# Fifteen small loads behind the last weights of a decode step, into a tile that nothing reads

## The chip, the cores and the metric

One Trainium2 chip, one of its cores. The metric is the device time of one execution in microseconds; a kernel's time is the median over its runs. The profile is one execution taken by the hardware profiler; its times count from the first instruction.

## What is computed

One decode step for two sequences (B = 2, one token each, D = 576), a sliding-window attention and a dense squared-ReLU layer side by side on the same normalised input:

```python
xn = _layernorm(x)
# attention: 32 query heads, 16 cached heads of 128, the last W = 2048 positions of the caches
q = (xn @ wq)                       # heads of 128
p = softmax(q k^T * 128 ** -0.5)
attn = (p v) @ wo
# dense layer, F = 4608
h = relu(xn @ w1 + b1) ** 2
dense = h @ w2 + b2
out = x + attn + dense
```

All inputs and the output are bf16. The caches' windows, 2 x 16 heads x 2048 positions x 128 for keys and for values, and the four weight matrices make up nearly all of the bytes: the profile counts 53.6 MB read from memory.

## The kernel before, in words

The attention is cut into eight units `u`: four groups of four cached heads, times two sequences. A unit has one 2 MB key tile and one 2 MB value tile (`issue_kv`, L106), each one DMA over 128 partitions. The order of the work on an engine is the order of the program: `step(u)` transposes the keys of a unit on TensorE, takes scores and softmax, and weights the values of unit `u - 2` in between. `mlp_h` makes the hidden layer from w1 after `step(6)`. At the end stand `step(NU - 1)`, the last two units' values (`pv_all`), and the output products: `out_acc` adds wo, then w2 in two halves, into one PSUM tile `out_ps`. `fin_sb` (L456) is its copy in SBUF, and the store at L457 writes the result. An earlier store (L455) of the same bytes to `out` takes its data from w2b; the later one writes over it.

All large loads are issued by SP, in one queue: first keys, wq and values, as buffers become free; then w1; then, after `mlp_h`, wo (L119), the first half of w2 (w2a, L438), and the second half in four pieces: nine row groups (w2b, L439), then six, two and one into the tile w2c (L441). x, b1, b2 and the two stores are issued by ACT.

The framework places the waits. DMAs of both queues complete on eight semaphores, given out in rotation in the order in which the framework schedules them, so a DMA waits for the one that used its semaphore before. Where a transfer writes bytes that an earlier one writes or that an engine still reads, it waits for that too. The program ends on SP with waits for the semaphores of the DMAs, and then a barrier of all engines (the line of the kernel's end, L483 in the profile).

The loads at the end, as they stand:

```python
    nc.sync.dma_start(out=w2a_sb[:], in_=w2_rows[0])
    nc.sync.dma_start(out=w2b_sb[:], in_=w2_rows[1, :, 0:R9 * D])
    for r0, r1 in W2P:
        nc.sync.dma_start(out=w2c_sb[:, (r0 - R9) * D:(r1 - R9) * D], in_=w2_rows[1, :, r0 * D:r1 * D])
```

Of the kernel before, what the change touches and what calls it, by code (L numbers as in the profile page):

```python
# [9 lines left out]
BF16 = mybir.dt.bfloat16  # L10
# [6 lines left out]
def kernel(  # L17
# [14 lines left out]
    nc = tc.nc  # L32
    P = 128
# [53 lines left out]
    w2pool = ctx.enter_context(tc.tile_pool(name="w2pool", bufs=1))  # L87
# [92 lines left out]
    for t0, half, k0, n, pc in ((0, 0, 0, NK, 0), (0, 1, 0, NK, 1), (1, 0, 1, NK - 1, 1), (1, 1, 0, NK - 1, 0)):  # L180
# [11 lines left out]
                          in_=own[:].unsqueeze(2).to_broadcast([P, NC, WC]))  # L192
# [11 lines left out]
                          in_=ident[0:2 * NG4, 0:2 * NG4].rearrange("p (x g) -> p x g", g=NG4).unsqueeze(3)  # L204
# [53 lines left out]
    def transposes(u, g):  # L258
        k_f = k_tiles[u][:].bitcast(F32)
        kT_ps = psum.tile([P, JG * P], BF16, tag="kT", bufs=3, name=f"kT_ps_{u}_{g}")  # L260
        kT_f = kT_ps[:].bitcast(F32)
        for i in range(JG // 2):
            j = g * JG // 2 + i
            transpose(out=kT_f[:, i * P:(i + 1) * P], in_=k_f[:, j * P:(j + 1) * P], identity=ident_f[:])
        t, o = divmod(g, TG)
        if o == 0:
            kT_tiles[(u, t)] = ktpool.tile([P, TG * JG * P], BF16, tag="kT_sb", name=f"kT_{u}_{t}")
        kT = kT_tiles[(u, t)][:, o * JG * P:(o + 1) * JG * P]
        if g % 2 == 0:
            nc.scalar.copy(out=kT, in_=kT_ps[:])  # L270
        else:
            nc.vector.tensor_copy(out=kT, in_=kT_ps[:])  # L272

    def scores(u, t):
        tq, b = divmod(u, B)
        if t == 0:
            sc_tiles[u] = psum.tile([P, NJJ * 32], F32, tag="sc", bufs=2, name=f"sc_ps_{u}")
            matmul(sc_tiles[u][:], lhsT=far_h[:], rhs=is_h, start=True, stop=False, skip_group_check=True)
        sc_ps = sc_tiles[u]
        kT = kT_tiles.pop((u, t))[:].rearrange("p (j k c) -> p j k c", k=P, c=2)  # L280
        z = QZ * (1 - t)
        for c in range(2):
            for g in range(4):
                matmul(sc_ps[32 * g:32 * (g + 1), :], lhsT=qz[:, tq, b, c, z:z + SR],
                       rhs=kT[:, :, 32 * g:32 * (g + 1), c], start=False, stop=(t == NT - 1 and c == 1),
                       skip_group_check=True, tile_position=(0, 32 * g))

    def softmax(u):
        sc_ps = sc_tiles.pop(u)
        m1 = work.tile([P, 1], F32, tag="m1", name=f"m1_{u}")  # L290
        nc.vector.tensor_reduce(out=m1[:], in_=sc_ps[:], axis=AX.X, op=ALU.max)  # L291
        m2 = work.tile([P, NC], F32, tag="m2", name=f"m2_{u}")
        nc.vector.tensor_scalar(out=m2[:], in0=off[:], scalar1=m1[:, 0:1], scalar2=None, op0=ALU.add)  # L293
        gmax = work.tile([P, NC], F32, tag="gmax", name=f"gmax_{u}")
        nc.gpsimd.partition_all_reduce(gmax[:], m2[:], channels=P, reduce_op=ReduceOp.max)  # L295
        gown = work.tile([P, NC], F32, tag="gown", name=f"gown_{u}")
        bias = work.tile([P, 1], F32, tag="bias", name=f"bias_{u}")
        nc.vector.scalar_tensor_tensor(out=gown[:], in0=gmax[:], scalar=-scale, in1=own[:], op0=ALU.mult,  # L298
                                       op1=ALU.mult, accum_out=bias[:])
        p_sb = work.tile([P, NJJ * 32], BF16, tag="p_sb", bufs=1, name=f"p_{u}")  # L300
        o1 = keep.tile([P, Dh + 1], F32, tag="o1", name=f"o1_{u}")
        nc.scalar.activation(out=p_sb[:], in_=sc_ps[:], func=ACT.Exp, bias=bias[:, 0:1], scale=scale,  # L302
                             accum_out=o1[:, Dh:Dh + 1])
        pT = keep.tile([P, NJJ, SR], BF16, tag="pT", name=f"pT_{u}")
        nc.vector.transpose(out=pT[:].rearrange("p j r -> p (j r)"), in_=p_sb[:])  # L305
        pT_tiles[u] = pT
        o1_tiles[u] = o1
# [6 lines left out]
    def pv(u, part, parts):  # L314
        n = NJJ // parts
        if part == 0:
            o_tiles[u] = psum.tile([P, NS * Dh], F32, tag="o", name=f"o_ps_{u}")
        v = v_tiles[u][:].rearrange("p (t j s d) -> p j t s d", t=NT, s=2, d=Dh)
        for j in range(part * n, (part + 1) * n):
            g = j % 4  # L320
            matmul(o_tiles[u][32 * g:32 * (g + 1), :], lhsT=pT_tiles[u][:, j, :], rhs=v[:, j], start=(j < 4),
                   stop=(j >= NJJ - 4), skip_group_check=True, tile_position=(0, 32 * g))
        if part == parts - 1:
            pT_tiles.pop(u)

    def pv_end(u):
        tq, b = divmod(u, B)
        o_ps = o_tiles.pop(u)
        o1 = o1_tiles.pop(u)
        for k in range(NS):  # L330
            kw = dict(out=o1[:, 0:Dh], in0=o_ps[:, k * Dh:(k + 1) * Dh])
            if k == 0:
                nc.vector.tensor_scalar(scalar1=in_s[:, 0:1], scalar2=None, op0=ALU.mult, **kw)
            else:
                nc.vector.scalar_tensor_tensor(scalar=in_s[:, k:k + 1], in1=o1[:, 0:Dh], op0=ALU.mult, op1=ALU.add,  # L335
                                               **kw)

        def fin():
            op = psum.tile([P, Dh + 1], F32, tag="op", name=f"op_ps_{u}")
            pp = slice(32 * tq, 32 * (tq + 1))  # L340
            matmul(op[pp, :], lhsT=of_h[:], rhs=o1[:], start=True, stop=True, skip_group_check=True,
                   tile_position=(0, 32 * tq))
            linv = work.tile([P, 1], F32, tag="linv", name=f"linv_{u}")
            nc.vector.reciprocal(out=linv[pp, :], in_=op[pp, Dh:Dh + 1])
            om_t = work.tile([P, Dh], F32, tag="om", name=f"om_{u}")
            om = om_t[pp, :].rearrange("p (q r) -> p q r", r=WR)
            nc.vector.scalar_tensor_tensor(out=om, in0=op[pp, 0:Dh].rearrange("p (q r) -> p q r", r=WR),
                                           scalar=linv[pp, 0:1], op0=ALU.mult, op1=ALU.mult,
                                           in1=own_c[pp, :].unsqueeze(2).to_broadcast([32, WC, WR]))
            with nc.allow_low_precision(reason="sums of one term and zeros"):  # L350
                nc.vector.tensor_reduce(out=ws[pp, :, BS * b], in_=om.rearrange("p q r -> p r q"), axis=AX.X,  # L351
                                        op=ALU.add)

        return fin
# [32 lines left out]
    def step(u):  # L387
        fin = None
        w = u - 2
        with_pv = w >= 0  # L390
        for g in range(NG):
            transposes(u, g)
            if with_pv and g == 1:
                pv(w, 0, 2)
            if with_pv and g == 2:
                pv(w, 1, 2)
                fin = pv_end(w)
            if g == TG + 1:
                scores(u, 0)
            if g == TG + 2 and fin:  # L400
                fin()
        scores(u, 1)
        softmax(u)

    def pv_all(u):
        pv(u, 0, 1)
        pv_end(u)()
# [31 lines left out]
    nc.sync.dma_start(out=w2b_sb[:], in_=w2_rows[1, :, 0:R9 * D])  # L439
    for r0, r1 in W2P:  # L440
        nc.sync.dma_start(out=w2c_sb[:, (r0 - R9) * D:(r1 - R9) * D], in_=w2_rows[1, :, r0 * D:r1 * D])  # L441
    step(NU - 1)
    pv_all(NU - 2)
    pv_all(NU - 1)
# [43 lines left out]
```

## Time and profile before

| | |
|---|---|
| time, median of 2 runs | 134.19 us (134.15 to 134.24) |
| span of the profiled execution (first to last instruction) | 132.1 us |
| time of the profiled execution beside its span | the page gives the span alone; the median is 2.1 us above it |
| busy share of the span | PE 64%, DVE 48%, ACT 35%, POOL 4% |
| mean granted TensorE clock | 0.834 |
| bytes read, mean rate | 53.62 MB, 406 GB/s over the span |
| chain that ended last | DMA 78%, PE 15%, ACT 2%, the rest 1% and less each |

How to read the views: the chain that ended last is followed back from the last instruction, each step to what released it; its columns are start, length and what. The timeline has start, length, engine, line, operation, output and input of each instruction, and in brackets what ended the idle time before it. SPq and ACTq are the instructions by which SP and ACT hand over DMAs; their length is that of the issue, not of the transfer. In a row of waits stand who waited, for whom, how long in total, how often, and the longest. The rows of digits and of GB/s cut the stretch asked for into 40 equal slices.

### The profile page before, as it was taken

The page shows a single profiled execution, that of the slowest core. Times are in us where ns is not written, and L with a number is a line of the kernel's source. Part 1 is how long each engine was busy: PE and PEld are TensorE (multiplying, and loading weights), DVE is VectorE, ACT ScalarE, POOL GpSimd, SP SyncE. Part 2 cuts the span into 40 slices and gives each one's busy share as a digit, 9 for nine tenths or more (in the row PEclk, how much of TensorE's full clock was granted, in tenths as well). Part 3 has the DMA queues.
Part 4 walks back from the last instruction along what each step waited for, and adds up shares of the span by engine and source line. Part 5 has one row for each costly group of instructions (what it writes and reads, how often), then busy time and mean ns, then how long its engine had stood idle before and what let it go on. Part 6 is the DMA issues. An engine that isn't in the chain of part 4 may idle for free.

```text
span 132.1 us, 2285 instructions
## 1 busy us (share of the span) xinstructions
PE 84.6 (64%) x949; PEld 52.6 (40%) x949; DVE 63.2 (48%) x176; ACT 46.7 (35%) x67; POOL 4.9 (4%) x15
## 2 busy tenths in 40 slices
PE   0089319599589687697599787104819972739471
PEld 0069202286345353363455443002417640229360
DVE  7764400344557677396547687410075667550000
ACT  5725400339566085283256094200106632000000
POOL 5000000010010100100100100100000001000000
PEclk9999955959999999999779999855695999555955
DMA  4999899999999999999999999999999999899960
GB/s 160 397 437 526 369 388 442 422 432 432 429 432 422 442 417 427 437 432 437 432 427 414 437 488 402 445 424 405 427 427 442 468 435 458 376 408 418 418 255 1
DMA packets 3511, 53.76 MB, mean 407 GB/s; under 512 B 419, under 2 KB 558, under 8 KB 814
## 3 DMA queue, kind: packets, MB, share of 16 engines
q1 hardware_dynamic: 3456, 53.61, 95.2%
q8 instruction: 7, 0.11, 0.3%
q10 hardware_dynamic: 46, 0.02, 0.1%
q14 instruction: 2, 0.02, 0.0%
HBM read 53.62 MB, written 0.00 MB: 406 GB/s over the span
## 4 chain that ended last, share of the span: by engine, by line
DMA 78%; PE 15%; ACT 2%; SPq 1%; DVE 1%; issue 1%; ACTq 0%; DVEq 0%
DMA w<-in_B_w_dram 25%; DMA w2c<-in_B_w_dram 24%; DMA k<-in_A_k_cache_dram 16%; DMA wq<-in_A_wq_dram 13%; PE kT_ps L97 5%; PE h_ps L94 3%; PE q_ps L94 3%; PE sc_ps L94 2%; PE out_ps L94 1%; PE o_ps L94 1%; ACT kT L270 1%; DVE qrow L238 1%; SPq L106 0%; ACT qrow L238 0%; DVE qz L254 0%
## 5 line engine op out<-in xcount | busy, mean ns | idle before, releaser
L97 PE MATMUL kT_ps<-ident_f,k 128*128 128x128 f32 x256 | 41.4, 312 | 5.7 <-DMA k<-in_A_k_cache_dram 3.9
L97 PEld LDWEIGHTS kT_ps<-ident_f,k 128*128 128x128 f32 x256 | 32.9, 161 | 18.8 <-issue 9.9
L270 ACT COPY kT<-kT_ps 128x1024 bf16<-128x1024 bf16 x32 | 31.9, 1012 | 17.8 <-PE kT_ps L97 17.8
L272 DVE COPY kT<-kT_ps 128x1024 bf16<-128x1024 bf16 x32 | 21.8, 682 | 6.4 <-PE kT_ps L97 6.1
L94 PE MATMUL sc_ps<-kT,qz 128*32 128x512 bf16 x128 | 9.9, 388 | 6.7 <-DVE kT L272 4.7
L302 ACT ACTIVATE p<-sc_ps,bias 128x512 bf16<-128x512 f32 x8 | 5.5, 688 | 21.4 <-DVE gown L298 18.2
L94 PE MATMUL o_ps<-v,pT 128*32 128x512 bf16 x128 | 11.2, 429 | 0.0
L94 PEld LDWEIGHTS <-xnT 128*4 128x4 bf16 x108 | 3.5, 121 | 16.8 <-issue 15.2
L94 PE MATMUL h_ps<-w,xnT 128*4 128x288 bf16 x72 | 4.3, 429 | 8.0 <-DMA w<-in_B_w_dram 8.0
L305 DVE STREAM_TRANSPOSE pT<-p 128x512 bf16<-128x512 bf16 x8 | 5.7, 710 | 6.2 <-ACT p L302 6.2
L335 DVE SCALAR_TENSOR_TENSOR o<-o_ps,in_s,o 128x128 f32<-128x128 f32 x24 | 8.3, 345 | 0.4
L291 DVE TENSOR_REDUCE m<-sc_ps 128x1 f32<-128x512 f32 x8 | 5.5, 692 | 4.8 <-PE sc_ps L94 4.8
L375 DVE TENSOR_TENSOR hrow<-t 100x1152 bf16<-100x1152 f32 x2 | 2.6, 1355 | 9.6 <-ACT t L373 9.6
L94 PE MATMUL q_ps<-wq,xnT 128*4 128x512 bf16 x36 | 4.0, 627 | 4.9 <-DMA wq<-in_A_wq_dram 4.9
L295 POOL PARTITION_ALL_REDUCE gmax<-m x8 | 2.9, 367 | 104.9 <-DVE m L293 104.9
L94 PE MATMUL op_ps<-o,of_h 128*32 128x129 f32 x16 | 3.7, 316 | 4.6 <-DVE o L335 4.6
L456 ACT CAST fin_sb<-out_ps 113x144 bf16<-113x144 f32 x1 | 0.3, 280 | 17.9 <-PE out_ps L94 17.9
L94 PEld LDWEIGHTS <-qz 128*32 128x32 bf16 x128 | 2.1, 94 | 10.4 <-DVE kT L272 7.2
L97 PE MATMUL pro_ps<-ident,xn_sb 2*128 2x2 bf16 x5 | 0.9, 182 | 6.8 <-DVE xn_sb L171 6.5
L94 PEld LDWEIGHTS <-hT_sb 128*17 128x17 bf16 x144 | 3.4, 108 | 3.6 <-issue 3.5
L94 PE MATMUL out_ps<-wo,ws 128*17 128x144 bf16 x128 | 4.0, 325 | 1.2 <-DVE ws L351 1.2
L238 DVE CAST qrow<-q_ps 100x512 bf16<-100x512 f32 x1 | 0.7, 692 | 8.2 <-PE q_ps L94 8.2
(71 smaller groups left out, 57.4 us busy)
## 6 DMA issues: line engine op xcount, KB each, us to landing
k<-in_A_k_cache_dram SPq DMA_DIRECT2D x8, 2048.0 KB, 21.0
v<-in_A_v_cache_dram SPq DMA_DIRECT2D x8, 2048.0 KB, 21.5
w<-in_B_w_dram SPq DMA_DIRECT2D x1, 5184.0 KB
wq<-in_A_wq_dram SPq DMA_DIRECT2D x1, 4608.0 KB, 17.8
wo<-in_A_wo_dram SPq DMA_DIRECT2D x1, 4608.0 KB
w2a<-in_B_w_dram SPq DMA_DIRECT2D x1, 2592.0 KB, 26.9
w2b<-in_B_w_dram SPq DMA_DIRECT2D x1, 1296.0 KB
w2c<-in_B_w_dram SPq DMA_DIRECT2D x1, 864.0 KB
```

The costliest lines, as they stand in the source:

```text
L94: tc.keep_in_program_order(nc.tensor.matmul(*a, **k))
L97: tc.keep_in_program_order(nc.tensor.transpose(*a, **k))
L238: cp(out=qrow[:, k * QW:(k + 1) * QW].rearrange("p (i a d) -> p i a d", a=2, d=Dh), in_=q_ps[0:RB, k * QW // 2:(k + 1) * QW // 2].rearrang ...
L270: nc.scalar.copy(out=kT, in_=kT_ps[:])
L272: nc.vector.tensor_copy(out=kT, in_=kT_ps[:])
L291: nc.vector.tensor_reduce(out=m1[:], in_=sc_ps[:], axis=AX.X, op=ALU.max)
L295: nc.gpsimd.partition_all_reduce(gmax[:], m2[:], channels=P, reduce_op=ReduceOp.max)
L302: nc.scalar.activation(out=p_sb[:], in_=sc_ps[:], func=ACT.Exp, bias=bias[:, 0:1], scale=scale, accum_out=o1[:, Dh:Dh + 1])
L305: nc.vector.transpose(out=pT[:].rearrange("p j r -> p (j r)"), in_=p_sb[:])
L335: nc.vector.scalar_tensor_tensor(scalar=in_s[:, k:k + 1], in1=o1[:, 0:Dh], op0=ALU.mult, op1=ALU.add, **kw)
L375: nc.vector.tensor_tensor(out=h4[:, :, k * HB:(k + 1) * HB], in0=t4, in1=t4, op=ALU.mult)
L456: nc.scalar.copy(out=fin_sb[:], in_=out_ps[:])
```

## The change

Behind the last piece of w2, still ahead of `step(NU - 1)` in the program, a new tile `own_sb` of 104 bf16 columns is made, and SP issues fifteen loads into it: 15 rows of 100 elements, 14 rows of 96, and so on to 2 rows of 48, and at last 1 row of 41. Each takes the top left corner of w2 and writes it from row 0 and column 0 of the tile. Nothing reads the tile.

```diff
     for r0, r1 in W2P:
         nc.sync.dma_start(out=w2c_sb[:, (r0 - R9) * D:(r1 - R9) * D], in_=w2_rows[1, :, r0 * D:r1 * D])
+    own_sb = w2pool.tile([P, 104], BF16, name="own_sb")
+    for k in range(15, 0, -1):
+        n = 41 if k == 1 else 40 + 4 * k
+        nc.sync.dma_start(out=own_sb[0:k, 0:n], in_=B_w2[0:k, 0:n])
     step(NU - 1)
     pv_all(NU - 2)
     pv_all(NU - 1)
```

## The prediction

> **What bounds the kernel now.** I read the chain that ended last first, then the last microseconds of the timeline, then what SP waited for there, and last the first microseconds, which hold the only small load on rings with little in them.
>
> The chain from 95 us on (start, length, what):
>
> ```profile
> 95.41 0.34 SPq L119
> ...
> 95.80 0.42 SPq L438
> ...
> 96.28 0.42 SPq L439
> ...
> 96.74 31.12 DMA w2c<-in_B_w_dram
> 127.86 0.04 issue
> 127.90 1.36 PE out_ps L94 x36
> 129.27 0.02 issue
> 129.29 0.28 ACT fin_sb L456
> ```
>
> Weights are streaming until the end: SP has handed over wo, w2a, w2b and the first w2c piece by 97 us, and TensorE waits for the data until 127.86. After that stand 36 matmuls, one cast and the store. The timeline behind it:
>
> ```profile
> 128.95 0.10 PEld L94 LDWEIGHTS <-hT_sb 128*17 128x17 bf16 x3
> 129.29 0.28 ACT L456 CAST fin_sb<-out_ps 113x144 bf16<-113x144 f32 x1 [17.85 <-PE out_ps L94]
> 129.60 0.54 ACTq L457 DMA_DIRECT2D out_dram<-fin_sb  x1
> ```
>
> The weights of the last four matmuls load at 128.95, so the last piece of w2c has landed at about 128.9. What SP waits for behind its last load (L483, the kernel's end):
>
> ```profile
> SPq L483 <- DMA w2c<-in_B_w_dram: 27.4, 3, 26.8
> SPq L483 <- DMA out_dram<-fin_sb: 2.3, 1, 2.3
> SPq L483 <- DMA out_dram<-w2b: 0.3, 1, 0.3
> ```
>
> Here is the point that decides this case: the end of the kernel waits for DMAs one by one, whether or not an engine reads what they bring. The wait for the first w2c piece ends at 127.9 (26.8 of the 27.4 us); 0.3 for the early store and 0.6 for two more pieces take it to 128.9 with the waits' own time, and 2.3 more to 131.2. The span ends at 132.1, so 0.85 us of closing barrier follow the last landing. The page gives no separate time for the profiled execution; the median of the runs, 134.19, is 2.1 above the span, and I take those 2.1 us to lie around it unchanged.
>
> **The change, part by part.** Nothing is removed and no instruction of PE, DVE, ACT or POOL moves. In the built program's list, SP has 15 more DMAs behind the third w2c piece, and ACT's final store counts on another completion semaphore, whose earlier user, w2a, has landed long before. There are eight such semaphores, in rotation, and the list also names what each DMA waits for:
>
> (a) Load 1 (15 rows) waits only for the semaphore's earlier user, the last v block, v_7. SP issued the third w2c piece at 100.74, when v_6 had landed; 2.1 MB more at the 437 GB/s of the page's rate row take 4.8 us, so load 1 is issued at about 105.5. Its issue of some 0.4 us costs nothing: SP has only its own new loads behind it, and w2 streams until 128.9. If that cover were gone, 0.4 us. Its 15 packets stand behind w2c in the same rings. The last w2c piece is not delayed by what stands behind it; were the two to mix, 15 packets of at most 200 bytes beside 1,152-byte ones would cost less than 0.1 us on PE. It lands about 0.1 after the last piece: 129.0.
>
> (b) Loads 2 to 15 each wait for the load before them to have landed. All write rows from 0 and columns from 0 of the same tile, so each overwrites part of the last one, and the framework puts a wait on full completion between them. Seven of them wait for a rotation's earlier user as well (wo, w2b, the w2c pieces, the two stores). All these have landed when their turn comes; the latest is the final store (131.2), which load 10 waits for, some 9 hops after 129.0. So there are 14 hops in series, from landing to landing, with nothing beside them: by 131.2 the chip is otherwise done. What is queued behind them on SP is the end of the kernel, and every engine waits for that in the closing barrier.
>
> **The price of one hop** is the whole question. The trace has one complete hop of this kind, at the start of the kernel:
>
> ```profile
> 0.72 0.63 SPq L106 DMA_DIRECT2D k<-in_A_k_cache_dram  x1
> 0.73 0.56 ACTq L125 DMA_DIRECT2D xb_sb<-in_A_x_dram  x1
> 2.19 0.55 SPq L106 DMA_DIRECT2D k<-in_A_k_cache_dram  x1
> ```
>
> with SP's waits of the first 3 us:
>
> ```profile
> SPq L106 <- DMA xb_sb<-in_A_x_dram: 0.2, 1, 0.2
> ```
>
> The second k load shares x's semaphore and was released by its landing: issue of x at 0.73, landing, next issue at 2.19. That is 1.46 us for two rows of 1,152 bytes, issue, fetch, landing and wake-up together. The other isolated transfer is the final store: issued at 129.60, SP released at 131.2, 1.6 us.
>
> Bounds. From below: ACT issued b1's small loads in 0.31 (four in 1.27), against 0.56 for x, so a warmed-up issue may save 0.25: 1.46 - 0.25 = 1.21. From above: the new loads touch up to 14 rows, x two. The DMA rate between 0.7 and 2.7 us, in slices of 0.05, shows both kinds:
>
> ```profile
> GB/s 0 0 0 0 0 0 0 0 0 0 0 0 0 0 0 0 0 0 0 46 0 0 0 0 0 0 0 0 983 1311 655 328 328 983 655 0 0 0 0 0
> ```
>
> x's packets are in slice 20 (1.65, which is 0.92 after its issue began); the 128-row k load's begin in slice 29 (2.10, 1.38 after). If the 0.46 between them is the price of many rows, a hop of 14 rows costs 1.46 + 0.4 = about 1.87, and one of 1 row 1.4. The loads shrink from 14 rows to 1, so by that reading their mean (7.5 rows, 5.5 more than x, at 0.46/14 = 0.033 each) is 1.64. I take 1.55, midway between the plain x hop (1.46) and this one, and near the store's 1.6.
>
> 14 x 1.55 = 21.7. Sum: 129.0 + 21.7 + 0.85 = 151.55 as the span, + 2.1 = 153.7 us. The ends: 14 x 1.21 gives 148.9, 14 x 1.87 gives 158.1.
>
> The Trainium skill, page "DMA: Bandwidth & Descriptors", section "Anatomy of one DMA", gives a fixed cost of about 2.0 us for each DMA on the GpSimd path, most of it the receipt of the last write; by that figure the sum would be 129.0 + 28 + 0.85 + 2.1 = 160.0. The same page, "Latency and other measured facts", has about 0.8 us as the least that a tiny transfer over HBM can take, which would make it 143.2. The trace's 1.46 lies between and was measured on these queues, so it decides.
>
> **The rivals.**
>
> *Nobody waits (not slower).* The loads go out one behind the other, as w2a, w2b and w2c did (issues at 95.80, 96.28 and 96.74, 0.48 apart): 15 x 0.48 = 7.2 us, from 105.5 to 112.7, all under the w2 stream; the data land at 129.0 behind w2c, ahead of the store, and the time stays 134.2. For it speaks that no engine reads the tile. It decides as soon as a load may start while the last one is in flight. Against it stand the waits in the built program, and SP's 2.3 us at the end for a store which nothing reads either.
>
> *Only the rotation counts (slower, little).* If a load waited only for its semaphore's earlier user, loads 1 to 9 would be out by 129.0 plus a little, load 10 would wait for the store (131.2), and five more issues at 0.48 put load 15 at 133.6, landing at 135.1: 138.0 in all. For it: this is all that the large loads wait for. Against it: the list names both.
>
> *A dearer hop.* The early store, issued at 125.80 beside the stream, was not in until about 128.25, 2.45 us. At 2.45 the time is 129.0 + 34.3 + 0.85 + 2.1 = 166.3. Against it: the rings were full then and are empty here (under 1% DMA share after 129.3). It would need small packets to cost a great deal by themselves.
>
> *A cheaper hop.* With empty rings and a warm queue 1.21 or less: 148.9. For it: x's load ran beside a 2 MB load that had just been issued.
>
> **How the numbers follow.** Hop between 1.3 and 1.9 in series: 0.84, and 153.7 is its time. Dearer 0.07, cheaper 0.05, rotation only 0.02, nobody waits 0.02. The range reaches from 1.3 (129.0 + 18.2 + 2.95 = 150.1) to just over the row bound of 158.1: 150.0 to 158.5. A measurement of this kernel tells about 2% (2.7 us) from no change. Only the case in which nobody waits lies within that, at 0.02, and nothing here makes the kernel faster, which I leave 0.01; slower 0.97.
>
> **What would show it right or wrong.** Right: until 129.3 the profile is as it was, the cast at 129.3 and the store at 129.6; SP shows one issue from own_sb near 105.5 and 14 single ones after 129.0, about 1.55 apart, each ended by a wait for the load before; the span ends 0.85 after the last landing, near 151.5. The spacing tells of the price: if it shrinks from about 1.9 to 1.4 along the loads, the number of rows counts; if it is level, it doesn't. Wrong: own_sb issues bunched between 105 and 113, a cast later than 129.5 (then w2c was delayed), or a hop outside 1.3 to 1.9.

## The result, and the profile after

151.24 us (median of 150.99 and 151.48) against 134.19: 1.1265 times as long, 95% interval 1.1218 to 1.1313. The forecast was 153.7, its range 150.0 to 158.5.

The page of the changed kernel, its head and its row of memory rates in 40 slices of the span:

```profile
span 149.1 us, 2307 instructions
...
GB/s 168 475 396 476 375 426 422 435 422 433 426 444 431 422 426 426 426 444 429 431 457 467 383 433 404 440 435 466 457 405 412 434 403 397 95 2 1 1 1 0
```

Up to slice 34 it is the stream of before. Then nearly nothing moves for five slices of 3.7 us each: the added time is waiting, not bytes. The timeline of the end (start, length, engine, line, operation):

```profile
128.04 1.40 PE L94 MATMUL out_ps<-w2c,hT_sb 128*17 128x144 bf16 x36 [1.33 <-DMA w2c<-in_B_w_dram]
...
129.15 0.10 PEld L94 LDWEIGHTS <-hT_sb 128*17 128x17 bf16 x3 [0.16 <-issue]
129.34 17.93 SPq L445 DMA_DIRECT2D own_sb<-in_B_w_dram  x14
129.49 0.28 ACT L460 CAST fin_sb<-out_ps 113x144 bf16<-113x144 f32 x1 [16.88 <-PE out_ps L94]
129.80 0.54 ACTq L461 DMA_DIRECT2D out_dram<-fin_sb  x1
```

The result's own work ends where it did, 0.2 us later: cast at 129.49 (129.29 before), store at 129.80 (129.60). Beside it, SP issues fourteen loads from 129.34 on, over 17.93 us. What SP waits for, from 95 us on:

```profile
SPq L445 <- DMA own_sb<-in_B_w_dram: 36.6, 14, 23.1
...
SPq L487 <- DMA own_sb<-in_B_w_dram: 0.7, 1, 0.7
```

Fourteen waits of the new line for the new loads themselves: the longest, 23.1, is load 2 waiting for load 1, which stands behind the stream; the other thirteen share 13.5. The kernel's end (L487) no longer waits for the store, which landed long before, but for the last load.

The issues one by one, from narrow windows of SP's timeline: load 1, then loads 2 to 7, and the last two:

```profile
105.80 0.41 SPq L445 DMA_DIRECT2D own_sb<-in_B_w_dram  x1
...
129.34 0.33 SPq L445 DMA_DIRECT2D own_sb<-in_B_w_dram  x1
130.99 0.31 SPq L445 DMA_DIRECT2D own_sb<-in_B_w_dram  x1
132.62 0.30 SPq L445 DMA_DIRECT2D own_sb<-in_B_w_dram  x1
134.12 0.29 SPq L445 DMA_DIRECT2D own_sb<-in_B_w_dram  x1
135.50 0.28 SPq L445 DMA_DIRECT2D own_sb<-in_B_w_dram  x1
137.09 0.27 SPq L445 DMA_DIRECT2D own_sb<-in_B_w_dram  x1
...
145.89 0.23 SPq L445 DMA_DIRECT2D own_sb<-in_B_w_dram  x1
147.04 0.22 SPq L445 DMA_DIRECT2D own_sb<-in_B_w_dram  x1
```

The distance from one start to the next is a hop: 1.65 us for 14 rows, 1.63, 1.50, 1.38, 1.59 for 10 rows, then 1.32 falling to 1.15 for 2 rows. The mean of the 13 from 129.34 to 147.04 is 1.36; the last seven of them are under 1.3. The last wait of 0.7 ends about 148.2, and the span 0.9 later.

### The profile page after: what moved, and what is told of

Read it like the earlier page. It is cut to its first block, busy times and chain, and to the rows that moved or that the text cites. A ratio compares the mean times of both kernels' runs of the same rounds, so it can differ in the third digit from the quotient of the medians.

```text
span 149.1 us, 2307 instructions
## 1 busy us (share of the span) xinstructions
PE 84.5 (57%) x949; PEld 51.3 (34%) x949; DVE 63.2 (42%) x176; ACT 46.6 (31%) x67; POOL 4.9 (3%) x15
## 4 chain that ended last, share of the span: by engine, by line
DMA 68%; PE 14%; SPq 2%; DVE 1%; ACT 1%; issue 1%; ACTq 0%; DVEq 0%
DMA w<-in_B_w_dram 21%; DMA w2c<-in_B_w_dram 21%; DMA k<-in_A_k_cache_dram 14%; DMA wq<-in_A_wq_dram 12%; PE kT_ps L97 5%; PE h_ps L94 3%; PE q_ps L94 2%; PE sc_ps L94 2%; PE o_ps L94 1%; PE out_ps L94 1%; SPq L106 1%; DVE qrow L238 0%; ACT qrow L238 0%; DVE qz L254 0%; SPq L438 0%
## 5 line engine op out<-in xcount | busy, mean ns | idle before, releaser
L97 PE MATMUL kT_ps<-ident_f,k 128*128 128x128 f32 x256 | 40.8, 306 | 5.9 <-DMA k<-in_A_k_cache_dram 4.2
L97 PEld LDWEIGHTS kT_ps<-ident_f,k 128*128 128x128 f32 x256 | 31.6, 156 | 20.3 <-issue 9.0
L94 PE MATMUL sc_ps<-kT,qz 128*32 128x512 bf16 x128 | 10.5, 413 | 6.7 <-DVE kT L272 4.7
L94 PE MATMUL q_ps<-wq,xnT 128*4 128x512 bf16 x36 | 3.5, 565 | 5.0 <-DMA wq<-in_A_wq_dram 5.0
L333 DVE TENSOR_SCALAR o<-o_ps,in_s 128x128 f32<-128x128 f32 x8 | 2.7, 340 | 4.0 <-PE o_ps L94 4.0
```

What stands on the lines that cost most here:

```text
L94: tc.keep_in_program_order(nc.tensor.matmul(*a, **k))
L97: tc.keep_in_program_order(nc.tensor.transpose(*a, **k))
```

## The experiments

Each was run beside the kernel before on the same chip, which took 133.96 to 134.01 us in these runs. All changes are in the new lines alone.

**Take the overwriting away.** Each load gets rows of its own (15 + 14 + ... + 1 = 120 of the tile's 128):

```diff
+    r = 0
     for k in range(15, 0, -1):
         n = 41 if k == 1 else 40 + 4 * k
-        nc.sync.dma_start(out=own_sb[0:k, 0:n], in_=B_w2[0:k, 0:n])
+        nc.sync.dma_start(out=own_sb[r:r + k, 0:n], in_=B_w2[0:k, 0:n])
+        r += k
```

> The fifteen loads, same order, rows and bytes, but each into rows of its own (0 to 14, 15 to 28, and so on), so that none overwrites another; the waits on the semaphores' earlier users stay. Theory (the overwriting makes each load wait for the one before): the series is gone. Loads 1 to 12 are issued by about 131.1, load 13 waits for the final store (landed at 131.4 in the trace of the change), the last is issued at about 132.2 and lands 1.2 later; 136.4 us, between 136.0 and 137.2. Rival (a small DMA behind another on one queue is held back by the queue itself, overwriting or not): 151.2, with the spacing of the change. Rival (the loads' landings cost the end nothing): 134.2.

Measured: 135.92 us, 1.0148 times before (1.0131 to 1.0165). SP's timeline in two stretches (the load at 131.00 stands in both), and what the kernel's end (here L489) waits for:

```profile
128.71 2.58 SPq L446 DMA_DIRECT2D own_sb<-in_B_w_dram  x7
...
131.00 1.20 SPq L446 DMA_DIRECT2D own_sb<-in_B_w_dram  x4
...
SPq L489 <- DMA own_sb<-in_B_w_dram: 0.7, 3, 0.3
```

The last ten loads now go out some 0.3 to 0.4 us apart, once 0.6, with several in flight at once, and the last is issued at about 131.95 instead of 147.04. Of the 17 us that the change costs, all but 2 hang on the overwriting. The rest is what the rotation of semaphores and the end's waits leave: some loads still go out behind the stream, and the end still waits for them. With 0.9 from the last landing to the end of the span of 134.1, the last load lands at about 133.2, 2.0 behind the 131.2 of the store in the kernel before. The time is just below the expected range: the last load is issued some 0.25 earlier than expected, with no wait for the store to be seen. A queue that held back small loads by itself is ruled out.

**Is it the rows, or the time since the stream ended?** In the change both move together: the loads get smaller while the stream lies further back. First the opposite order:

```diff
-    for k in range(15, 0, -1):
+    for k in range(1, 16):
```

> The same loads in the opposite order, 1 row first and 15 rows last. The hops of the change shrank from 1.64 us (14 rows) to 1.15 (2 rows). Theory (a hop costs more the more rows it has): they now grow from about 1.15 to 1.65, and the time is 151.5 (the 15-row hop replaces the 1-row one). Rival (a hop gets cheaper the longer the weight stream has been over, whatever its rows): they shrink as before, 1.64 first and 1.15 last, 151.2. The spacing of the issues decides, not the total.

Measured: 149.30 us, ratio 1.1144 (1.1122 to 1.1167). The issues of the loads of 2, 3 and 4 rows, and of 14 and 15 rows:

```profile
127.77 0.25 SPq L445 DMA_DIRECT2D own_sb<-in_B_w_dram  x1
128.94 0.24 SPq L445 DMA_DIRECT2D own_sb<-in_B_w_dram  x1
130.15 0.25 SPq L445 DMA_DIRECT2D own_sb<-in_B_w_dram  x1
...
143.75 0.31 SPq L445 DMA_DIRECT2D own_sb<-in_B_w_dram  x1
145.23 0.32 SPq L445 DMA_DIRECT2D own_sb<-in_B_w_dram  x1
```

The hops grow, from 1.17 (2 rows) to 1.48 (14 rows), though not evenly (4 rows took 1.49, 6 to 10 rows 1.26 to 1.33), and the issue grows from 0.25 to 0.31. So the price does not fall with the time since the stream. The total missed by 2.2 us, for a reason that I had not thought of: load 1, now one row, is in by 127.77, ahead of the last w2c piece that stands before it in the queue (the last weights load at 129.04 in this trace). The series starts 1.6 us earlier than in the change, while the stream is still coming in.

Then all loads alike, one row each, and 15 rows each:

```diff
-        nc.sync.dma_start(out=own_sb[0:k, 0:n], in_=B_w2[0:k, 0:n])
+        nc.sync.dma_start(out=own_sb[0:1, 0:41], in_=B_w2[0:1, 0:41])      # or
+        nc.sync.dma_start(out=own_sb[0:15, 0:100], in_=B_w2[0:15, 0:100])
```

> All fifteen loads take one row of 41 elements into the same place. Theory (rows set the price): 14 hops of about 1.17 us, level, so 129.1 + 16.4 + 0.85 + 2.1 = 148.5. Rival (price falls with time since the stream): shrinking hops, 151.2.

> All fifteen loads take 15 rows of 100 elements into the same place. Theory (rows set the price): 14 hops of about 1.66 us, level, so 129.3 + 23.2 + 0.85 + 2.1 = 155.5. Rival (price falls with time since the stream): shrinking hops, about 151.2 to 152.

Measured: 147.23 us for one row (ratio 1.0990, 1.0959 to 1.1022) and 153.54 for 15 (1.1461, 1.1437 to 1.1486). Loads 2 to 15 on SP's timeline, with one row:

```profile
127.64 15.52 SPq L444 DMA_DIRECT2D own_sb<-in_B_w_dram  x14
```

and with 15 rows:

```profile
129.25 20.03 SPq L444 DMA_DIRECT2D own_sb<-in_B_w_dram  x14
```

The length runs from the first issue's start to the last one's end, so less one issue (0.22 and 0.32) it is 13 hops: 1.18 us each with one row, 1.52 with 15. Single hops lie within 1.15 to 1.33 and 1.45 to 1.64, with no fall along the series. The direction was right and two sizes were off: 15 rows cost 1.52 and not 1.66, and the one-row series starts at 127.64 and not at 129.1, as in the opposite order. The rows differ in length too, 82 bytes and 200; one row of 200 bytes was not tried.

**Rows, or the engines that carry them?** 17 rows, and 128 rows:

```diff
-        nc.sync.dma_start(out=own_sb[0:k, 0:n], in_=B_w2[0:k, 0:n])
+        nc.sync.dma_start(out=own_sb[0:17, 0:100], in_=B_w2[0:17, 0:100])      # or
+        nc.sync.dma_start(out=own_sb[0:128, 0:100], in_=B_w2[0:128, 0:100])
```

> All fifteen loads take 17 rows of 100 elements into the same place. One-row loads had hops of 1.16 us and landed their first at 127.6; 15-row loads 1.52 and 129.2. Theory A (what costs is the number of rows): 1.16 + 16 x 0.026 = 1.57, first landing 129.2, so 129.2 + 22.0 + 0.85 + 2.1 = 154.2. Theory B (what costs is the number of DMA engines that a load is spread over; 17 rows, a prime above 16, go to a single one, as the Trainium skill has it): the first load lands near 127.7 as the one-row load did, and a hop is that of one row plus 16 more short packets, 1.3 to 1.4: 127.7 + 18.9 + 2.95 = 149.6.

> All fifteen loads take 128 rows of 100 elements into the same place. Theory A (rows): 1.16 + 127 x 0.026 = 4.5 a hop, 129.3 + 63 + 2.95 = 195. Theory B (engines: sixteen, with eight packets each): 1.6 to 1.7 a hop, 129.3 + 23.1 + 2.95 = 155.4.

Measured: 151.28 us for 17 rows (1.1287, 1.1266 to 1.1307), 156.15 for 128 (1.1651, 1.1629 to 1.1672). With 17 rows:

```profile
127.75 19.55 SPq L444 DMA_DIRECT2D own_sb<-in_B_w_dram  x14
```

and with 128 rows:

```profile
129.33 22.76 SPq L444 DMA_DIRECT2D own_sb<-in_B_w_dram  x14
```

A price for each row is ruled out: 128 rows cost 1.73 a hop, not 4.5, a little over the 1.6 to 1.7 of the other theory. 17 rows lie between the two expectations. Their first load is in at 127.75, as with one row (127.64) and unlike 15 or 128 rows (129.25, 129.33), and the profile has the issue at 0.225 us, as for one row (0.223), against 0.323 for 15 rows and 0.328 for 128. So much speaks for a single engine. The Trainium skill, page "DMA: Bandwidth & Descriptors", section "Why a DMA increments its semaphore by 16 and not by 1", says that a load is split over the largest number of engines up to 16 that divides the outermost size (sizes of 1 left out) of both source and target, and so a prime above 16 over one; these numbers agree with it. But the hop is 1.49, not 1.3 to 1.4. The rate row of one such hop, 1.2 us from its issue in slices of 0.03, shows the packets one after the other:

```profile
GB/s 0 0 0 0 0 0 0 0 0 0 0 0 0 0 0 0 0 0 0 0 0 0 0 0 0 0 0 0 7 13 20 13 13 20 13 13 0 0 0 0
```

They begin in slice 29, at least 0.84 after the issue began, one slice behind the single packet of a one-row hop (slice 28 in its rate row below), and take eight slices, 0.24 us: that is most of the 0.31 between 1.18 and 1.49. One engine saves the longer issue and pays it back in packets.

**Are the first loads free?** Only load 1 and load 2 are kept:

```diff
-    for k in range(15, 0, -1):
+    for k in range(15, 13, -1):
```

> Only the first two loads of the change, 15 rows and 14 rows. Theory: the second lands at about 131.0, ahead of the final store (131.4), so both are covered and the time is that of before, 134.0, at most 0.2 more if the last w2c piece is held up. Rival (each load behind w2c costs the end its hop): 135.5 with one hop, 137 with two.

Measured: 134.19 us against 134.01, ratio 1.0012 (1.0003 to 1.0021). SP's waits from 128 us on:

```profile
SPq L445 <- DMA own_sb<-in_B_w_dram: 23.1, 1, 23.1
SPq L487 <- DMA out_dram<-fin_sb: 1.6, 1, 1.6
```

The end waits for the store again, and not for load 2. The second load lies beside the cast and the store. In the trace of the change the third is issued at 130.99 and the fourth, which waits for its landing, at 132.62, behind the store; so the change pays from the third on. The 0.18 us that remain go with the last matmuls, whose weights load at 129.11 here and at 128.95 before. The 15 packets of load 1 do not explain it: in the one-row series, where load 1 is a single row, these weights load as late, at 129.12. The first w2c piece is already later here, its matmuls starting at 128.06 against 127.90. Why the stream stands a little later stays open.

**The hop that the prediction started from.** x's load, two rows of 1,152 bytes, fifteen times (in a tile from the pool of the caches, for room):

```diff
-    own_sb = w2pool.tile([P, 104], BF16, name="own_sb")
+    own_sb = kvpool.tile([P, D], BF16, tag="kv", name="own_sb")
     for k in range(15, 0, -1):
-        n = 41 if k == 1 else 40 + 4 * k
-        nc.sync.dma_start(out=own_sb[0:k, 0:n], in_=B_w2[0:k, 0:n])
+        nc.sync.dma_start(out=own_sb[0:2, :], in_=x2d)
```

> All fifteen loads take two rows of 1,152 bytes, the load of x whose hop of 1.46 us the prediction started from (that one was issued by ACT as its first, beside a 2 MB load). Theory (the 1.46 holds a cold issue and the company of the large load, not the size): hops of 1.15 to 1.2, as the two-row load of the change; 128.0 + 14 x 1.18 + 2.95 = 147.5. Rival (bytes: two rows of 1,152 cost 1.46 wherever they stand): 128.0 + 20.4 + 2.95 = 151.4.

Measured: 149.81 us, ratio 1.1178 (1.1153 to 1.1202), halfway between the two. On the timeline:

```profile
128.35 17.30 SPq L444 DMA_DIRECT2D own_sb<-in_A_x_dram  x14
```

(17.30 - 0.23) / 13 = 1.31 a hop. So of x's 1.46, some 0.15 were its place at the start of the kernel, on ACT's queue (the issue took 0.56 there and takes 0.23 here, but the rest of the hop was 0.18 shorter there), and some 0.15 more its longer rows, against 1.15 for the change's two short rows. Neither theory had it alone.

**What a hop is made of.** One row again, but from a tile in SBUF:

```diff
-        nc.sync.dma_start(out=own_sb[0:k, 0:n], in_=B_w2[0:k, 0:n])
+        nc.sync.dma_start(out=own_sb[0:1, 0:41], in_=xb_sb[0:1, 0:41])
```

> The one-row experiment again, but the 82 bytes come from a tile in SBUF that is ready long before (xb_sb) and not from memory. With the source in memory a hop was 1.16 us, and the trace showed its packet 0.83 us after the issue began and the landing 0.3 after the packet. Theory (the hop is issue, preparation and completion; the read of memory is a small part): 1.05 to 1.16 a hop, 127.6 + 14 x 1.1 + 2.95 = 146.0, up to 147.2. Rival (reading memory is what takes the time): under 0.9 a hop, 143.2 or less.

Measured: 151.84 us, ratio 1.1331 (1.1298 to 1.1364): slower than from memory (147.23), which neither side expected. Its loads 2 to 15:

```profile
127.77 20.30 SPq L444 DMA_DIRECT2D own_sb<-xb_sb  x14
```

The rate row of one of its hops, 1.2 us from the issue at 139.94 in slices of 0.03:

```profile
GB/s 0 0 0 0 0 0 0 0 0 0 0 0 0 0 0 0 0 0 0 0 0 0 0 0 0 0 0 0 0 0 0 0 0 0 0 0 0 0 0 3
```

The same row with the source in memory, from an issue at 138.26:

```profile
GB/s 0 0 0 0 0 0 0 0 0 0 0 0 0 0 0 0 0 0 0 0 0 0 0 0 0 0 0 3 0 0 0 0 0 0 0 0 0 0 0 0
```

A hop is 1.52 us from SBUF and 1.18 from memory; the issue takes 0.54 and 0.22, and the packet follows in slice 40 (1.17 after the issue began) and slice 28 (0.81). So both stages behind the issue are alike, about 0.6 from its end to the packet and 0.35 from the packet to the next issue, and nearly the whole difference is in handing the transfer over. Two thirds of a hop or more pass before the packet starts. Why the hand-over is longer was not tried.

## Why the prediction was right, and where it was off

The time lies inside the range, 1.2 us above its low end. The mechanism is shown; the price inside it was set too high, and two errors in it partly cancel.

*The end waits for loads that nobody reads.* Right: SP's L487 waits for own_sb in the trace of the change, and with two loads alone it waits for the store.

*Fourteen hops in series.* Right, and shown by taking the overwriting away: of 17.05 us, 15 go. The rival in which only the rotation counts, priced at 138.0, is what that experiment makes real, and it came out at 135.9: its price was too high because the loads go out some 0.35 us apart and not 0.48, the last one lands 1.2 us after its issue and not 1.46, and no load of that kernel shows a wait for the store, where the rival had load 10 wait for it.

*Load 1 lands at 129.0, w2c is not delayed.* Load 2 is issued at 129.34, so the first term was 0.3 short. 0.2 of it is the last w2c piece itself, later in this trace (129.15 against 128.95, the first piece already by 0.14); the rest is the landing behind it. That load 1 lands behind w2c holds for its 15 rows; one row behind the same stream was in by 127.64, before the last piece. The 0.4 us issue at 105.80 costs nothing, as said (105.5).

*The price of a hop, 1.55.* This is the term that was mis-sized: 1.36 in the trace, and 14 times 0.19 is 2.7 us, against an error of 2.5 in all (the first term gives 0.3 back). The base was too high. The x hop was taken whole, 1.46, with its place at the start and its long rows, where the short two-row load measures 1.15; the lower bound of 1.21, which took the cold issue off, was the better start. The final store, cited as a near row, was of another kind: it goes out of SBUF, and in the load from SBUF even one small row costs 1.52. The share for the rows was too low, which hid part of this: the prediction put 0.09 on the x hop, half of its 0.18 for 5.5 more rows, and the trace has about 0.2 between its mean of 1.35 and the two-row hop. That the error was not larger is in part luck.

How the price goes with the rows was right in direction. The prediction read 0.46 for 14 more rows off the 128-row load at the start. Level series give 0.34 from one row to 15, and 0.55 from one row to 128: an extra that is soon reached, not a price by row, and an uneven one (the hops of 14 to 10 rows lie between 1.38 and 1.65, the last of them up again at 1.59; in that of 10 rows the trace has one packet of 0.33 us among others of 0.01).

*The signs named beforehand.* The cast at 129.49 stays just inside the 129.5 named. The spacing shrinks along the loads, as said for the case that rows count, but from 1.65 to 1.15 and not from 1.9 to 1.4. A hop outside 1.3 to 1.9 was named as a sign of being wrong, and the last seven of the thirteen hops measured are such, 1.28 to 1.15; the mean of 1.36 is not.

*The sum by what was measured:* 129.3 + 14 x 1.35 + 0.9 = 149.1, the span. The 2.1 us around it was 0.2 too much: this execution took 150.99, 1.9 above its span, as the kernel before does in the 25 runs beside the experiments (1.84 to 1.98). The other execution, 151.48, had a span of 149.6, and the median lies between the two.

*The page's 2.0 us for a DMA* (Trainium skill, "DMA: Bandwidth & Descriptors", "Anatomy of one DMA", for the GpSimd path) would have given 160.0; no series here had a mean above 1.73. Its account, for that path, that the completion is most of the cost is not what these loads on SP's queue show: in the one-row hop the packet comes 0.8 us after the issue began, and the rest takes 0.35. The 0.8 us that the same page has as the least for a tiny transfer is not contradicted; the shortest hop here is 1.15.

## What to carry to other kernels

A load that nobody reads is free only as long as nothing waits for it, and here two things did: the next load, because both wrote the same bytes, and the end of the kernel. Look for small transfers that overwrite each other's targets: here each paid 1.2 to 1.7 us in full, one after the other, while the same transfers to bytes of their own went out 0.35 us apart. And price a hop by a warm transfer of the same kind, same source, same queue, small rows, not by the first DMA of the kernel.

## What the runs showed of the hardware that I had not expected

A load of one row, or of 17, issued behind the stream, was in by 127.6 to 127.8, before the last piece issued ahead of it (129.0 to 129.2): on this queue, issued later was not landed later. A load of 82 bytes from SBUF took SP 0.54 us to hand over, as many bytes from memory 0.22. And 128 rows of 200 bytes cost only 0.2 us more per hop than 15.
